# Wider products for the scores and for y in a chunked RWKV-7 kernel, and a refit of its scheduler

## The chip, the cores and the metric

The kernel runs on one core of one Trainium2 chip. The metric is the device time of one execution in microseconds (us). Runs of a kernel spread by up to 3% here, so kernels are compared by ratios of fast runs that were timed in the same rounds on the same chip.

## The reference

Batch 4, 8 heads, 768 steps, 40 channels per head; then a feed-forward block over 3072 tokens, 320 to 2048 to 320.

```python
for t in range(S):
    y[:, :, t] = np.einsum('bhd,bhde->bhe', rt, state)
    Sa = np.einsum('bhde,bhe->bhd', state, at)
    state = (state * wt[:, :, None, :] - np.einsum('bhd,bhe->bhde', Sa, bt)
             + np.einsum('bhd,bhe->bhde', vt, kt))
# y as (3072, 320) is x
h = x @ w_in
out = (h / (1.0 + np.exp(-1.702 * h))) @ w_out
```

## The kernel before

The recurrence is solved in chunks of 64 steps. A *unit* is one chunk of two batches (16 heads); there are 24. Every product of a unit is f32 on quarters of the array (64 rows by 64 columns), four tiles side by side: `QUARTERS` names them. Each call of `mm` becomes two passes, and each pass is a weight load and a matmul, so four instructions: the 16 calls of `score_RV` in each of the 24 units are the 768 matmuls of ps_RV below, with 768 loads. "Weights" here means the stationary operand, `lhsT`.

For y, each unit makes score matrices: v against r (`score_RV`) and SA against r (`scores`; SA is the solution of the chunk's triangular system). Both are masked by DVE, and `read` multiplies them with the decayed k and b. In the same product come 40 columns for the state: v's own values and those of SA.

```python
def mm(o, lhsT, rhs, start):
    nc.tensor.matmul(o, lhsT, rhs, start=start, stop=True, skip_group_check=True)

def by_time(t):                     # cumulative sum by time
    ps, lw = psum(t, "ps_cum"), logw_of(i)
    for n in (1, 0):
        for b in BITS:
            u = b ^ n
            mm(ps[HALF[u], b, :160], incl[HALF[b]], lw[HALF[b], n * 160:(n + 1) * 160], True)

def score_RV(t):                    # v against r; ready early, long before y
    for e, b in product(BITS, BITS):
        for f, u in QUARTERS:
            o, j = (2 * e + b) * 64, 4 * u + 2 * e + b
            mm(ps[HALF[u], f, o:o + 64], rv[HALF[f], 1, j], rv[HALF[f], 0, j], o == 0)
# ... DVE masks it into RV

# ... level(n, b): six levels of the triangular solve; in the last one each quarter
# writes its own half, mm(ps[HALF[q], h, ...], ...), 40 columns

def scores(t):                      # SA against r
    for e, b in product(BITS, BITS):
        for f, u in QUARTERS:
            o = (2 * e + b) * 64
            mm(ps[HALF[u], f, o:o + 64], saT_of(i)[HALF[f], 4 * e + 2 * u + b], rT[HALF[f], 4 * u + 2 * e + b], o == 0)
# ... DVE masks it into M

def read(t):                        # y and the new state
    for b, f in product(BITS, BITS):
        o = (2 * b + f) * 104
        for m, w in ((RV_of(i), kh_of(i)), (M_of(i), bh_of(i))):
            for u, e in QUARTERS:
                mm(ps[HALF[e], u, o:o + 104], w[HALF[u], 4 * b + 2 * f + e], m[HALF[u], 4 * f + 2 * e + b],
                   o == 0 and w is kh_t[i % 2])
```

The matmuls of the feed-forward block (`ps_up`, `ps_down`) fill TensorE between the steps of the solve. A small scheduler in the host code orders all this before it is emitted. It simulates every engine and the fetch of TensorE's instructions (`FETCH` ns for 256 of them, more beside transfers: `BESIDE`), with a duration given for each task; the numbers such as `pe((4, 64))` are these durations and not hardware settings.

## Time and profile before

| | before |
|---|---|
| time, first 3 runs | 824.3, 842.7, 842.1 us |
| time, medians of four later sets (11 to 59 runs) | 829.7 to 836.2 us |
| profiled span | 826.5 us |
| TensorE passes (loads and matmuls each) | 24,192 |
| instruction fetches of TensorE | 190 |

The prediction shows the main lines of the page and says what each is for. Two more belong to the change. They are from the table of groups; the columns are line, engine, operation, output<-inputs, shape, count, then busy us, mean ns of one, and the idle time before them.

```profile
L270 PE MATMUL ps_RV<-rv 64*64 64x64 f32 x768 | 18.0, 227 | 3.4 <-issue 2.1 <-ACT G L498 1.3
L270 PE MATMUL ps_M<-rv,saT 64*64 64x64 f32 x768 | 16.8, 218 | 0.4 <-ACT saT L641 0.4
```

`64*64 64x64` says that the array is used as a tile of 64 rows by 64 columns, with 64 moving columns. The reader should not take the mean of 218 ns for a cost: four tiles overlap, and neighbours start 14.5 ns apart on average.

### The profile page before, as it was taken

The page shows a single profiled execution, that of the slowest core. Times are in us where ns is not written, and L with a number is a line of the kernel's source. Part 1 is how long each engine was busy: PE and PEld are TensorE (multiplying, and loading weights), DVE is VectorE, ACT ScalarE, POOL GpSimd, SP SyncE. Part 2 cuts the span into 40 slices and gives each one's busy share as a digit, 9 for nine tenths or more (in the row PEclk, how much of TensorE's full clock was granted, in tenths as well). Part 3 has the DMA queues.
Part 4 walks back from the last instruction along what each step waited for, and adds up shares of the span by engine and source line. Part 5 has one row for each costly group of instructions (what it writes and reads, how often), then busy time and mean ns, then how long its engine had stood idle before and what let it go on. Part 6 is the DMA issues. An engine that isn't in the chain of part 4 may idle for free.

```text
span 826.5 us, 51261 instructions
## 1 busy us (share of the span) xinstructions
PE 754.0 (91%) x24192; PEld 630.7 (76%) x24192; DVE 477.3 (58%) x757; ACT 368.8 (45%) x634; POOL 148.2 (18%) x208
## 2 busy tenths in 40 slices
PE   4764898999899998999998998999999999999997
PEld 3664788887787786889787777788789888778664
DVE  7479898745754645546556456566466566455100
ACT  4564754443436347346445435344256445233110
POOL 4020303321312302302203212022113022100000
PEclk9896999999999999999999999999999999999999
DMA  9935433332411512323323315134133223110100
GB/s 343 336 116 165 167 121 110 108 104 54 151 56 58 149 59 78 117 75 94 112 73 101 110 43 157 36 94 133 56 97 113 64 68 105 49 36 29 35 10 17
DMA packets 33018, 82.60 MB, mean 100 GB/s; under 512 B 5128, under 2 KB 11272, under 8 KB 31528
## 3 DMA queue, kind: packets, MB, share of 16 engines
q1 hardware_dynamic: 32808, 79.32, 30.2%
q8 instruction: 190, 3.11, 1.5%
q14 instruction: 20, 0.16, 0.1%
HBM read 71.43 MB, written 7.86 MB: 96 GB/s over the span
## 4 chain that ended last, share of the span: by engine, by line
PE 84%; ACT 5%; DVE 4%; issue 4%; DMA 2%; SPq 0%; POOL 0%; ACTq 0%; POOLq 0%
PE ps_up L270 24%; PE ps_down L270 23%; PE ps_level L270 18%; PE ps_y L270 5%; PE ps_N L270 2%; PE ps_NT L270 2%; PE ps_A L270 2%; PE ps_rz L270 1%; PE ps_saT L270 1%; PE ps_M L270 1%; PE ps_zT L270 1%; PE ps_Av L270 1%; PE ps_RV L270 1%; ACT g L835 1%; ACT W L714 1%
## 5 line engine op out<-in xcount | busy, mean ns | idle before, releaser
L270 PE MATMUL ps_up<-xT,w_sb 64*64 64x256 f32 x3840 | 271.1, 380 | 8.5 <-ACT g L835 3.4
L270 PE MATMUL ps_down<-w_sb,g 64*64 64x320 f32 x3072 | 244.0, 431 | 1.7 <-DVE ob L861 0.6
L270 PEld LDWEIGHTS ps_up<-xT,w_sb 64*64 64x64 f32 x3840 | 155.6, 134 | 32.6 <-issue 6.6
L270 PEld LDWEIGHTS ps_level<-W,E 64*64 64x64 f32 x5888 | 149.2, 134 | 29.6 <-ACT g L835 3.5
L714 ACT COPY W<-ps_level 128x672 f32<-128x672 f32 (+1 forms) x154 | 95.2, 621 | 164.2 <-PE ps_level L270 152.1
L270 PEld LDWEIGHTS ps_down<-w_sb,g 64*64 64x64 f32 x3072 | 123.1, 134 | 46.3 <-issue 2.4
L270 PE MATMUL ps_level<-W,E 64*64 64x64 f32 (+2 forms) x5888 | 146.6, 230 | 6.4 <-DVE E L704 1.7
L709 DVE TENSOR_TENSOR E<-twice,ps_level 128x512 f32<-128x512 f32 x120 | 81.5, 683 | 64.7 <-ACT W L714 54.1
L535 POOL TENSOR_TENSOR kh<-time,G 128x320 f32<-128x320 f32 x22 | 19.6, 891 | 454.8 <-issue 254.6
L270 PEld LDWEIGHTS ps_level<-W 64*64 64x64 f32 x2560 | 69.9, 142 | 20.9 <-issue 12.6
L270 PE MATMUL ps_level<-W 64*64 64x64 f32 (+2 forms) x2560 | 71.9, 243 | 14.1 <-issue 10.4
L835 ACT ACTIVATE g<-ps_up 128x1024 f32<-128x1024 f32 x48 | 49.2, 1025 | 60.0 <-PE ps_up L270 59.6
L799 POOL TENSOR_TENSOR x<-y,FT 128x128 f32<-128x128 f32 x84 | 48.0, 601 | 19.7 <-DMA b<-in_b 19.6
L693 DVE TENSOR_TENSOR W<-edge,ps_level 128x672 f32<-128x672 f32 x40 | 34.0, 851 | 23.7 <-PE ps_level L270 21.1
L270 PE MATMUL ps_y<-RV,kh 64*64 64x104 f32 x768 | 38.5, 263 | 9.6 <-DVE M L756 9.1
L861 DVE TENSOR_TENSOR ob<-ob,ps_down 128x320 f32<-128x320 f32 x24 | 11.6, 484 | 58.8 <-ACT ob L859 58.4
L270 PEld LDWEIGHTS ps_y<-RV,kh 64*64 64x64 f32 x768 | 30.7, 142 | 12.6 <-DVE M L756 9.5
L270 PE MATMUL ps_y<-M,bh 64*64 64x104 f32 x768 | 38.7, 263 | 0.2 <-issue 0.2
L714 DVE COPY W<-ps_level 128x672 f32<-128x672 f32 (+1 forms) x46 | 34.4, 750 | 6.7 <-PE ps_level L270 6.7
L527 POOL TENSOR_TENSOR ak<-ak,FT 128x512 f32<-128x512 f32 x21 | 28.2, 1341 | 27.1 <-DMA ak<-in_ak 16.2
L756 DVE TENSOR_TENSOR M<-ps_M,upper 128x512 f32<-128x512 f32 x24 | 16.5, 688 | 26.5 <-PE ps_M L270 26.4
L859 ACT COPY ob<-ps_down 128x320 f32<-128x320 f32 x24 | 10.2, 426 | 47.1 <-PE ps_down L270 46.9
(111 smaller groups left out, 1019.6 us busy)
## 6 DMA issues: line engine op xcount, KB each, us to landing
time<-in_time SPq DMA_DIRECT2D x24, 480.0 KB
RV<-in_v SPq DMA_DIRECT2D x24, 416.0 KB
xT<-x_dram SPq DMA_DIRECT2D x48, 160.0 KB
ak<-in_ak SPq DMA_DIRECT2D x44, 160.0 KB
rv<-in_rv SPq DMA_DIRECT2D x44, 160.0 KB
wc<-in_wc SPq DMA_DIRECT2D x24, 264.0 KB
extra<-in_w_out SPq DMA_DIRECT2D x4, 1024.0 KB
logw<-in_w SPq DMA_DIRECT2D x24, 160.0 KB
```

The source lines that it names most:

```text
L270: nc.tensor.matmul(o, lhsT, rhs, start=start, stop=True, skip_group_check=True)
L527: plan.add(R, {"DVE": 690.0, "POOL": 1270.0, "sbuf": True}, lambda t: of(t.engine).tensor_mul(ahT(), ahT(), FT_of(i)), reads=T("ak", "FT") ...
L535: plan.add(R + 4, {"POOL": 870.0, "DVE": 490.0, "sbuf": True}, lambda t, n=n, dst=dst: of(t.engine).tensor_mul(dst(i)[:, :, :D], by_head(t ...
L693: plan.add(key, dve(672), lambda t: nc.vector.tensor_sub(W_of(s + 1)[:, :, b], edge[:, :, b], item(t)[:, :, :, :168]), reads=T("edge"), wr ...
L709: plan.add(key, dve(512), lambda t: nc.vector.tensor_sub(E_of(es + 1)[:, :, b].rearrange("p h j (n t) -> p h (j n) t", n=2), wide(twice).t ...
L714: plan.add(key, any2(4 * (168 - lo)), lambda t: copy(t.engine)(W_of(s + 1)[:, :, b, :, lo:], item(t)[:, :, :, lo:168]), writes=keeps, pair ...
L756: plan.add(R + 4, dve(512), lambda t: nc.vector.tensor_tensor(M_of(i)[:, :, :64].rearrange("p (e j) t -> p e j t", e=2), psum(t, "")[:, :, ...
L799: of(t.engine).tensor_mul(x[:, b ^ u, b], y_of()[:, at], FT_of(i)[:, at])
L835: plan.add(-45, act(1024), lambda t: nc.scalar.activation(g_of(c * NQ + q).rearrange("p m r n -> p r m n"), psum(t, "").rearrange("p r (m ...
L859: plan.add(-45, any2(320), lambda t: copy(t.engine)(ob_of(serial), psum(t, "")[:, 0, :DM]), writes=[("ob", serial)], pair=("down", serial))
L861: plan.add(-45, dve(320), lambda t: nc.vector.tensor_add(ob_of(serial), ob_of(serial), psum(t, "")[:, 1, :DM]), reads=[("ob", serial)], wr ...
```

## The change

Its intent is fewer TensorE instructions. v and SA lie side by side in one tile (`rv`, three planes: r, v, SA), so one load of 128 columns makes both scores of a head. Their results land on the two halves of the partitions, so y becomes one product over 128 rows. For that, the last level has to write only to the upper half, and the decay G has to exist on both halves for both batches. v is loaded without zeros, and the scheduler's constants are fitted anew. The cut diff leaves out that the masks are re-laid, that k and b are decayed in one product of 640, and that `xT` has two buffers in place of three.

```diff
-    BLOCK, FETCH, BESIDE, AHEAD = 256, 3550.0, 0.4, 300.0
-    DELAY = {"PE": 300.0, ... "SP": 800.0}
-    LATENCY, RATE, SPREAD = 1200.0, 400.0, 1.3
+    BLOCK, FETCH, BESIDE, AHEAD = 256, 3550.0, 0.37, 300.0
+    DELAY = {"PE": 300.0, ... "SP": 1300.0}
+    LATENCY, RATE = 1200.0, 400.0
...
-    W_IN, W_OUT = 12, 30
+    W_IN, W_OUT = 12, 35
...
         def by_time(t):
-            for n in (1, 0):
-                for b in BITS:
-                    u = b ^ n
-                    mm(ps[HALF[u], b, :160], incl[HALF[b]], lw[HALF[b], n * 160:(n + 1) * 160], True)
+            for b, h in QUARTERS:
+                mm(ps[HALF[h], b, :DM], incl[HALF[b]], lw[HALF[b]], True)
...
-        def score_RV(t): ...            # removed
...
+                        if last:
+                            o = (2 * q + j) * 128
+                            mm(ps[HALF[1], h, o:o + D], E[HALF[h], q, j, 64:], w[HALF[h], q, j, 64:104], j == 0 and q == h)
+                            continue
...
         def scores(t):
-            for e, b in product(BITS, BITS):
-                for f, u in QUARTERS:
-                    mm(ps[HALF[u], f, o:o + 64], saT_of(i)[HALF[f], ...], rT[HALF[f], ...], o == 0)
-        plan.add(R + 4, pe((4, 64)), scores, ...)
+            for j, (b, e, u) in enumerate(product(BITS, BITS, BITS)):
+                for f in BITS:
+                    mm(ps[:, f, j * 64:(j + 1) * 64], rv[HALF[f], 4 * e + 2 * b + u, 1:].rearrange("p r t -> p (r t)"),
+                       rv[HALF[f], 4 * e + 2 * b + u, 0], j == 0)
+        plan.add(R + 4, {"PE": 930.0 + 290.0, "instr": 64}, scores, ...)
...
         def read(t):
-            for m, w in ((RV_of(i), kh_of(i)), (M_of(i), bh_of(i))):
-                for u, e in QUARTERS:
-                    mm(ps[HALF[e], u, o:o + 104], w[HALF[u], ...], m[HALF[u], ...], ...)
+            for b, f, u, e in product(BITS, BITS, BITS, BITS):
+                mm(ps[HALF[e], u, o:o + 104].rearrange("p (g n) -> p g n", n=8), kb_of(i)[:, 8 * b + head(e, f, b, u)],
+                   RM_of(i)[:, :, 8 * b + 4 * e + 2 * u + f], o == 0)
+        plan.add(R + 4, {"PE": 1435.0 + 290.0, "instr": 64}, read, ...)
```

More of the change, by code (lines that the diff above doesn't have):

```diff
@@ L59 @@
 class Plan:
-    BLOCK, FETCH, BESIDE, AHEAD = 256, 3550.0, 0.4, 300.0
-    DELAY = {"PE": 300.0, "DVE": 60.0, "ACT": 60.0, "POOL": 150.0, "SP": 800.0}
-    LATENCY, RATE, SPREAD = 1200.0, 400.0, 1.3
+    BLOCK, FETCH, BESIDE, AHEAD = 256, 3550.0, 0.37, 300.0
+    DELAY = {"PE": 300.0, "DVE": 60.0, "ACT": 60.0, "POOL": 150.0, "SP": 1300.0}
+    LATENCY, RATE = 1200.0, 400.0
     def __init__(self, slots, pairs):
@@ L125, in fetch @@
                 beside = sum(max(0.0, min(y, at + took) - max(x, at)) for x, y in running[-8:])
-                took = self.FETCH + self.BESIDE / self.SPREAD * beside
+                took = self.FETCH + self.BESIDE * beside
             return took
@@ L178, in order @@
                 wire = max(wire, end + self.LATENCY)
-                running.append((wire, wire + self.SPREAD * t.size / self.RATE))
+                running.append((wire, wire + t.size / self.RATE))
                 end = wire = running[-1][1]
@@ L248, in rwkv7_gelu_quick @@
     banks = ctx.enter_context(tc.tile_pool(name="banks", bufs=1, space=bass.MemoryType.PSUM))
-    plan = Plan(dict(logw=3, wc=3, G=1, wch=3, wz=2, time=2, ak=2, b=2, rv=2, FT=3, GT=1, kh=2, bh=2, bz=2,
-                     A=1, Av=1, RV=2, W=3, E=2, edge=1, zraw=2, zT=1, saT=1, M=2, y=1, x=1, xT=3, g=4, ob=1), 4)
+    plan = Plan(dict(logw=3, wc=3, G=1, wch=3, wz=2, time=2, ak=2, b=2, rv=2, FT=3, GT=1, kb=2, bz=2,
+                     A=1, Av=1, RM=2, W=3, E=2, edge=1, zraw=2, zT=1, saT=2, y=1, x=1, xT=2, g=4, ob=1), 4)
     tiles, psums, drams = {}, {}, {}
@@ L336, in several @@
         return [single(f"{name}{i}", shape) for i in range(plan.slots[name])]
-    kh_t, bh_t = several("kh", [128, 8, 64]), several("bh", [128, 8, 64])
-    for t in kh_t + bh_t:
+    kb_t = several("kb", [128, 16, 64])
+    for t in kb_t:
         nc.gpsimd.memset(t[:, :, D:], 0.0)
@@ L343, in rwkv7_gelu_quick @@
         nc.gpsimd.memset(t[:, DM:], 0.0)
-    ak_t, b_t, rv_t = several("ak", [128, 2, 8, 64]), several("b", [128, 8, 64]), several("rv", [128, 2, 8, 64])
+    ak_t, b_t, rv_t = several("ak", [128, 2, 8, 64]), several("b", [128, 8, 64]), several("rv", [128, 8, 3, 64])
     bz_t = several("bz", [128, 8 * 104 + 24])
@@ L420, in weights @@
             weight(n, W_IN + 0.4 * n if n < NK else W_OUT + 1.6 * (n - NK), w_in[n] if n < NK else w_out[n - NK])
-    time_of = lambda i: buf("time", i, [128, 3, DM])
+    time_of = lambda i: buf("time", i, [128, 3 * DM])
     ak_of, b_of, rv_of = lambda i: ak_t[i % 2], lambda i: b_t[i % 2], lambda i: rv_t[i % 2]
-    RV_of = lambda i: buf("RV", i, [128, 8, 104])
+    RM_of = lambda i: buf("RM", i, [128, 13, 16, 8])
     logw_of = lambda i: buf("logw", i, [128, DM])
@@ L437, in load, with go @@
         for name, of, src, n in (("ak", ak_of, ak_d, 1024), ("time", time_of, time_d, 3 * DM), ("b", b_of, b_d, 512),
-                                 ("rv", rv_of, rv_d, 1024), ("RV", RV_of, v_d, 832)):
+                                 ("rv", rv_of, rv_d, 1024), ("RM", RM_of, v_d, 640)):
             rows = [slice(p.start, p.start + D) for p in HALF] if i >= 2 and name in ("ak", "b", "rv") else [slice(0, 128)]
-            def go(t, of=of, src=src, rows=rows):
+            def go(t, name=name, of=of, src=src, rows=rows):
+                if name == "RM":
+                    nc.sync.dma_start(of(i)[HALF[0], 8:].rearrange("p g j n -> p (g j n)"), src[i])
+                    return
                 for p in rows:
-                    nc.sync.dma_start(of(i)[p], src[i, p])
-            plan.add(10 * i - 4, {"SP": 350.0 * len(rows)}, go, writes=[(name, i)] + ([("v", i)] if name == "RV" else []),
-                     size=sum(p.stop - p.start for p in rows) * n * 4)
-    G_of = lambda i: buf("G", i, [128, 2, 160])
+                    nc.sync.dma_start(of(i)[p, :, :2] if name == "rv" else of(i)[p], src[i, p])
+            plan.add(10 * i - 4, {"SP": 350.0 * len(rows)}, go, writes=[(name, i)],
+                     size=128 * n * (5.5 if name == "rv" else 2 if name == "RM" else 4))
+    G_of = lambda i: buf("G", i, [128, 2, DM])
     FT_of = lambda i: buf("FT", i, [128, 8, 64])
@@ L478, in by_time @@
             ps, lw = psum(t, "ps_cum"), logw_of(i)
-            for n in (1, 0):
-                for b in BITS:
-                    u = b ^ n
-                    mm(ps[HALF[u], b, :160], incl[HALF[b]], lw[HALF[b], n * 160:(n + 1) * 160], True)
-        plan.add(R, pe((1, 160)), by_time, reads=T("log"), uses=T("logw"), room=T("G"), writes=T("cum"), pair=("cum", i))
+            for b, h in QUARTERS:
+                mm(ps[HALF[h], b, :DM], incl[HALF[b]], lw[HALF[b]], True)
+        plan.add(R, pe((1, 320)), by_time, reads=T("log"), uses=T("logw"), room=T("G"), writes=T("cum"), pair=("cum", i))
         def exp_channel(t):
@@ L497, in decay @@
                  writes=T("FT", "GT", "wch"))
-        plan.add(R, {"ACT": 460.0}, lambda t: nc.scalar.activation(G_of(i), psum(t, "")[:, :, :160], ACT.Exp, scale=-1.0),
+        plan.add(R, {"ACT": 700.0}, lambda t: nc.scalar.activation(G_of(i), psum(t, "")[:, :, :DM], ACT.Exp, scale=-1.0),
                  reads=T("FT"), writes=T("G", "exps"), pair=("cum", i))
@@ L503, in decay @@
                      reads=T("wch") + [("wch", i - 2)], writes=T("wz"))
-    def by_head(t):
-        return t.rearrange("t (h d) -> t h d", h=H)
     A_of = lambda i: buf("A", i, [128, 8, 64])
@@ L513, in rwkv7_gelu_quick @@
     zraw_of = lambda i: buf("zraw", i, [128, 8, D])
-    saT_of = lambda i: buf("saT", i, [128, 8, 64])
-    M_of = lambda i: buf("M", i, [128, 8, 104])
     xT_of = lambda c: buf("xT", c, [128, 2, NK, 128])
-    kh_of, bh_of = lambda i: kh_t[i % 2], lambda i: bh_t[i % 2]
+    kb_of = lambda i: kb_t[i % 2]
     zT_of = lambda i: zT_t[i % plan.slots["zT"]]
@@ L523, in prep @@
         T = lambda *names: [(n, i) for n in names]
-        G = lambda: G_of(i).rearrange("t b (h d) -> t (b h) d", d=D)
         ahT, khT = (lambda: ak_of(i)[:, 0]), (lambda: ak_of(i)[:, 1])
@@ L533, in prep @@
                  reads=T("ak", "GT"), writes=T("khT"))
-        for n, (name, dst) in enumerate((("kh", kh_of), ("bh", bh_of))):
-            plan.add(R + 4, {"POOL": 870.0, "DVE": 490.0, "sbuf": True}, lambda t, n=n, dst=dst: of(t.engine).tensor_mul(
-                dst(i)[:, :, :D], by_head(time_of(i)[:, n]), G()), reads=T("time", "exps", "G"), writes=T(name))
+        plan.add(R + 4, {"POOL": 1700.0, "DVE": 830.0, "sbuf": True}, lambda t: of(t.engine).tensor_mul(
+            kb_of(i)[:, :, :D], time_of(i)[:, :2 * DM].rearrange("t (h d) -> t h d", d=D),
+            G_of(i).rearrange("t b (h d) -> t (b h) d", d=D)), reads=T("time", "exps", "G"), writes=T("kb"))
         def score_NT(t):
@@ L563, in times_v @@
         def times_v(t):
-            ps, v_b = psum(t, "ps_Av"), time_of(i)[:, 2]
+            ps, v_b = psum(t, "ps_Av"), time_of(i)[:, 2 * DM:]
             for e, f in product(BITS, BITS):
@@ L573, in prep @@
                  writes=T("Av"), pair=("Av", i))
-        def score_RV(t):
-            ps, rv = psum(t, "ps_RV"), rv_of(i)
-            for e, b in product(BITS, BITS):
-                for f, u in QUARTERS:
-                    o, j = (2 * e + b) * 64, 4 * u + 2 * e + b
-                    mm(ps[HALF[u], f, o:o + 64], rv[HALF[f], 1, j], rv[HALF[f], 0, j], o == 0)
-        plan.add(R + 9, pe((4, 64)), score_RV, reads=T("rv"), room=T("RV"), pair=("RV", i))
-        plan.add(R + 9, dve(512), lambda t: nc.vector.tensor_tensor(
-            RV_of(i)[:, :, :64].rearrange("p (e j) t -> p e j t", e=2), psum(t, "")[:, :, :256].rearrange("p e (j t) -> p e j t", t=64),
-            mask(upper), ALU.mult), reads=T("v"), writes=T("RV"), pair=("RV", i))
     def last_e(i):
@@ L682, in level @@
             wide = lambda t: t.unsqueeze(1).unsqueeze(1)
-            sets = [(2, 104 if n < LEVELS - 2 else 40)] + ([] if last else [(2, 64)]) + ([(1, 80)] if early and alone else [])
+            sets = [(2, 104 if n < LEVELS - 2 else 120 if last else 40)] + ([] if last else [(2, 64)]) + ([(1, 80)] if early and alone else [])
             key, pair = R + 1 + n * 0.5, (f"L{b}", s)
@@ L686, in level @@
                      uses=[("W", s)] + ([] if alone else [("E", es)]),
-                     room=T("M") if last else [("W", s + 1)] + ([] if early and n < LEVELS - 2 else [("E", es + 1)]), pair=pair)
+                     room=T("RM") if last else [("W", s + 1)] + ([] if early and n < LEVELS - 2 else [("E", es + 1)]), pair=pair)
             keeps = [(f"W{b}", s + 1), ("W", s + 1)]
@@ L698, in level @@
             elif last:
-                plan.add(key, any2(160), lambda t: signed(
-                    t, M_of(i).rearrange("p (f e b) n -> p b e f n", f=2, e=2)[:, b, :, :, 64:], item(t)[:, :, :, 64:104], i >= EARLY),
-                         writes=T("M"), pair=pair)
+                plan.add(key, any2(320), lambda t: signed(
+                    t, RM_of(i)[HALF[1], 8:, 8 * b:8 * b + 8].rearrange("p g j n -> p j g n"),
+                    psum(t, "")[HALF[1]].rearrange("p h (j n) -> p (h j) n", n=128)[:, :, :D].rearrange("p j (g n) -> p j g n", n=8),
+                    i >= EARLY), writes=T("RM"), pair=pair)
             else:
@@ L723, in sa_turned @@
             ps, w, E = psum(t, "ps_saT"), W_of(6 * i + 5), E_of(last_e(i))
-            for u, b in product(BITS, BITS):
+            for b, u in product(BITS, BITS):
                 for e, f in QUARTERS:
-                    o = (2 * u + b) * 64
+                    o = (2 * b + u) * 64
                     mm(ps[HALF[f], e, o:o + 64], w[HALF[e], u, b, f, 64:128], E[HALF[e], u, b, f, 64:], o == 0)
@@ L731, in solve @@
         plan.add(R + 4, any2(512), lambda t: signed(
-            t, saT_of(i).rearrange("p (r j) t -> p r (j t)", r=2), psum(t, "")[:, :, :256], i >= EARLY), writes=T("saT"), pair=("saT", i))
+            t, rv_of(i)[:, :, 2].rearrange("p (e j) t -> p e j t", e=2),
+            psum(t, "")[:, :, :256].rearrange("p e (j t) -> p e j t", t=64), i >= EARLY), writes=T("saT"), pair=("saT", i))
         y_of, x_of = lambda: buf("y", i, [128, 8, 64]), lambda: buf("x", i, [128, 4, 2, 64])
@@ L736, in read_state @@
             def read_state(t):
-                ps, rT = psum(t, "ps_rz"), rv_of(i)[:, 0]
+                ps, rT = psum(t, "ps_rz"), rv_of(i)[:, :, 0]
                 for u, b in product(BITS, BITS):
@@ L741, in read_state @@
                         o, at = (2 * u + b) * 64, (4 * e + 2 * u + b) * D
-                        mm(ps[HALF[e], f, o:o + 64], zT_of(i)[HALF[f], at:at + 64], rT[HALF[f], 4 * u + 2 * e + b], o == 0)
+                        mm(ps[HALF[e], f, o:o + 64], zT_of(i)[HALF[f], at:at + 64], rT[HALF[f], 4 * e + 2 * b + u], o == 0)
             plan.add(R + 6, pe((4, 64)), read_state, reads=T("rv", "zT"), room=T("y"), pair=("rz", i))
@@ L748, in scores @@
         def scores(t):
-            ps, rT = psum(t, "ps_M"), rv_of(i)[:, 0]
-            for e, b in product(BITS, BITS):
-                for f, u in QUARTERS:
-                    o = (2 * e + b) * 64
-                    mm(ps[HALF[u], f, o:o + 64], saT_of(i)[HALF[f], 4 * e + 2 * u + b], rT[HALF[f], 4 * u + 2 * e + b], o == 0)
-        plan.add(R + 4, pe((4, 64)), scores, reads=T("saT", "rv"), room=T("M"), pair=("M", i))
-        plan.add(R + 4, dve(512), lambda t: nc.vector.tensor_tensor(
-            M_of(i)[:, :, :64].rearrange("p (e j) t -> p e j t", e=2), psum(t, "")[:, :, :256].rearrange("p e (j t) -> p e j t", t=64),
-            mask(upper), ALU.mult), writes=T("M"), pair=("M", i))
+            ps, rv = psum(t, "ps_M"), rv_of(i)
@@ new lines, in scores @@
+            for j, (b, e, u) in enumerate(product(BITS, BITS, BITS)):
+                for f in BITS:
+                    mm(ps[:, f, j * 64:(j + 1) * 64], rv[HALF[f], 4 * e + 2 * b + u, 1:].rearrange("p r t -> p (r t)"),
+                       rv[HALF[f], 4 * e + 2 * b + u, 0], j == 0)
+        plan.add(R + 4, {"PE": 930.0 + 290.0, "instr": 64}, scores, reads=T("saT", "rv"), room=T("RM"), pair=("M", i))
+        for f in BITS:
+            plan.add(R + 4, dve(512), lambda t, f=f: nc.vector.tensor_tensor(
+                RM_of(i)[:, :8].rearrange("p g (j f) n -> p f j g n", f=2)[:, f],
+                psum(t, "")[:, f].rearrange("p (j g n) -> p j g n", j=8, g=8),
+                upper.rearrange("p (g n) -> p g n", n=8).unsqueeze(1).to_broadcast([128, 8, 8, 8]), ALU.mult),
+                     writes=T("RM"), pair=("M", i))
@@ L760, in read @@
         def read(t):
             ps = psum(t, "ps_y")
-            for b, f in product(BITS, BITS):
+            for b, f, u, e in product(BITS, BITS, BITS, BITS):
                 o = (2 * b + f) * 104
-                for m, w in ((RV_of(i), kh_of(i)), (M_of(i), bh_of(i))):
-                    for u, e in QUARTERS:
-                        mm(ps[HALF[e], u, o:o + 104], w[HALF[u], 4 * b + 2 * f + e], m[HALF[u], 4 * f + 2 * e + b],
-                           o == 0 and w is kh_t[i % 2])
-        plan.add(R + 4, pe((8, 104)), read, reads=T("RV", "M", "kh", "bh") + (T("rz") if c > 0 else []), room=T("y", "zraw"),
-                 pair=("y", i))
+                mm(ps[HALF[e], u, o:o + 104].rearrange("p (g n) -> p g n", n=8), kb_of(i)[:, 8 * b + head(e, f, b, u)],
+                   RM_of(i)[:, :, 8 * b + 4 * e + 2 * u + f], o == 0)
@@ L772, in part @@
+        plan.add(R + 4, {"PE": 1435.0 + 290.0, "instr": 64}, read, reads=T("RM", "kb") + (T("rz") if c > 0 else []),
+                 room=T("y", "zraw"), pair=("y", i))
         def part(t):
@@ L813, in get_back @@
                 nc.sync.dma_start(xT_of(c)[h, p].rearrange("q k n -> q (k n)"), drams[i].rearrange("(q k) n -> q (k n)", q=64))
-        plan.add(-50, {"SP": 700.0}, part_with, reads=T("x"), writes=T("xd"), size=DM * 512)
+        plan.add(-50, {"SP": 700.0}, part_with, reads=T("x"), writes=T("xd"), size=DM * 512 * 1.6)
         plan.add(-50, {"SP": 700.0}, get_back, reads=T("xd"), writes=[("xT", c), ("xs", (c, p))], size=2 * DM * 512)
@@ L905, with by_batch, time_tile, both @@
     units = [(c, p) for c in range(NC) for p in range(B // 2)]
-    def time_tile(x, swapped):
-        x = np.asarray(x, np.float32).reshape(B, H, NC, C, D)
-        t = np.empty((len(units), 2, C, H, D), np.float32)
-        for n, (c, p) in enumerate(units):
-            for half in range(2):
-                for slot in range(2):
-                    if swapped:
-                        hs = 4 * (slot ^ half)
-                        t[n, half, :, 4 * slot:4 * slot + 4] = x[2 * p + slot, hs:hs + 4, c].transpose(1, 0, 2)
-                    else:
-                        t[n, half, :, 4 * slot:4 * slot + 4] = x[2 * p + half, 4 * slot:4 * slot + 4, c].transpose(1, 0, 2)
-        return t.reshape(len(units), 128, H * D)
+    def by_batch(x):
+        x = np.asarray(x, np.float32).reshape(B // 2, 2, H, NC, C, D).transpose(3, 0, 1, 4, 2, 5)
+        return x.reshape(len(units), 2, C, H, D)
+    def time_tile(x):
+        return by_batch(x).reshape(len(units), 128, H * D)
+    def both(x):
+        return by_batch(x).transpose(0, 2, 1, 3, 4).reshape(len(units), C, 2 * H * D)
     def channel_tile(x, half, order):
@@ L935, in beside @@
         x = np.asarray(x, np.float32).reshape(B, H, NC, C, D)
-        t = np.zeros((len(units), 2, C, 8, C + D), np.float32)
+        t = np.empty((len(units), C, D // 8, 16, 8), np.float32)
         for n, (c, p) in enumerate(units):
             for e, f, b, u in product(range(2), repeat=4):
-                t[n, u, :, 4 * f + 2 * e + b, C:] = x[2 * p + b, e + 2 * f + 4 * (b ^ u), c]
-        return t.reshape(len(units), 128, 8, C + D)
+                t[n, :, :, 8 * b + 4 * e + 2 * u + f] = x[2 * p + b, e + 2 * f + 4 * (b ^ u), c].reshape(C, D // 8, 8)
+        return t.reshape(len(units), C, 16 * D)
     def halves(t):
@@ L956 @@
     arrays = {
-        "in_time": np.ascontiguousarray(np.stack([time_tile(k, True), time_tile(b, True), time_tile(v, False)], 2)),
+        "in_time": np.concatenate([np.concatenate([both(k), both(b)], 1), time_tile(v)], 2),
         "in_v": beside(v),
-        "in_w": time_tile(w, False),
+        "in_w": np.ascontiguousarray(time_tile(w)),
         "in_wc": halves(channel_tile(w, "e", "ubf")),
@@ L962 @@
         "in_b": channel_tile(b, "e", "ubf"),
-        "in_rv": np.ascontiguousarray(np.stack([channel_tile(r, "f", "ueb"), channel_tile(v, "f", "ueb")], 2)),
+        "in_rv": np.ascontiguousarray(np.stack([channel_tile(r, "f", "ebu"), channel_tile(v, "f", "ebu")], 3)),
         "in_w_in": np.ascontiguousarray(w_in),
```

## The prediction

> **What bounds the kernel now.** I read the page first: busy table, slices, chain by engine, DMA queues.
>
> ```profile
> PE 754.0 (91%) x24192; PEld 630.7 (76%) x24192; DVE 477.3 (58%) x757; ACT 368.8 (45%) x634; POOL 148.2 (18%) x208
> ...
> PE   4764898999899998999998998999999999999997
> ...
> q8 instruction: 190, 3.11, 1.5%
> ...
> PE 84%; ACT 5%; DVE 4%; issue 4%; DMA 2%; SPq 0%; POOL 0%; ACTq 0%; POOLq 0%
> ```
>
> TensorE is the bound from about 140 us on; no other engine is near it. It reads 48,384 instructions (each f32 product is two passes, each pass a weight load and a matmul), and the queue line shows how they come: in 190 fetches, 3.11 MB, so 16 KiB or 256 instructions each. In the trace the starts of these fetches lie 3.9 us apart in the median, 3.4 us at the lowest tenth. TensorE needs about as long to use a block up, so there are two bounds side by side: array time and fetch.
>
> The windows table says where TensorE is not full:
>
> ```profile
> 0.00:70.00 70.00, 38.83 (x1472) 35.26 (x1472) 48.53 (x75) 36.49 (x64) 14.25 (x31) 0.91 0.68 247
> 70.00:140.00 70.00, 59.34 (x2008) 53.39 (x2012) 61.86 (x79) 40.50 (x64) 19.26 (x20) 0.89 0.46 148
> 140.00:759.00 619.00, 593.16 (x19444) 501.09 (x19440) 359.69 (x590) 279.83 (x489) 114.68 (x157) 0.99 0.29 87
> 759.00:827.00 68.00, 62.70 (x1284) 40.98 (x1276) 7.24 (x16) 11.98 (x19) 0.00 (x0) 0.99 0.08 21
> ```
>
> For array time I take durations from the timeline, start of one set to start of the next:
>
> ```profile
> 159.90 0.68 PE L270 MATMUL ps_RV<-rv 64*64 64x64 f32 x32
> 160.36 1.07 PE L270 MATMUL ps_up<-xT,w_sb 64*64 64x256 f32 x16
> ```
>
> So 32 passes of 64 columns take 0.46 us: 14.5 ns each, four tiles of the array sharing 58 ns. The same reading gives 22.3 ns for a pass of 104 columns (64 in 1.43 us, the ps_y pieces of the chain) and 67.5 ns for 320 columns (16 in 1.08 us, ps_down). With these,[...] all 24,192 passes sum to **712 us** of pure array time. Walking the starts of all matmuls with those costs leaves 91 us in which the array had nothing queued: 50 us before 140 us, 40 us between 140 and 759. When I number TensorE's instructions, 32 of the 81 us in the larger of these gaps fall into one sixteenth of the 256 positions of a block: these are waits for **fetch**. The waits view shows the same under "issue":
>
> ```profile
> PE ps_level L270 <- issue: 11.8, 10, 3.5
> PE ps_y L270 <- DVE M L756: 9.1, 1, 9.1
> ```
>
> The second line is start-up: DVE, converting weights, was late with a mask once.
>
> [...]every form on the page is 64*64. [...]The trace has only 64-column loads (134 ns recorded, overlapped). [...]the 128x512 masks (687 and 688 ns) agree, so I expect the re-laid masks to cost the same.
>
> **The change part by part**, per unit (24 units).
>
> Fewer instructions. v's score product, 32 passes, disappears into the one of SA; y goes from 64 passes to 32. That is 64 passes, 128 instructions per unit, 3,072 in all: 12 fetches fewer, 178.
>
> Scores. Before: two products of 32 passes, 2 x 0.464 = 0.93 us. After: 32 passes with 128 loaded columns on two row tiles, not four: if a tile's pass still takes 58 ns, 16 x 58 = 0.93 us, the same. [...]I take the first, which is also the entry in the scheduler's table, with 0.29 us for switching the tiling: **+0.29 us**.
>
> y. Before 64 x 22.3 = 1.43 us on four tiles; after 32 passes on two tiles of 128 rows, 44.7 ns each, again 1.43, with a switch: **+0.29 us**.
>
> Last level. All its outputs now go to the upper half of the partitions, so two tiles work instead of four: 2 x 16 passes go from 0.46 us to 0.82 (the table's 51.5 ns per pair of passes): **+0.36 us**.
>
> Cumulative sum by time. Every half now needs both batches: 8 passes of 320 columns in place of 160, 0.54 for 0.27: **+0.27 us**.
>
> Sum +1.21 us per unit, **+29 us**: array time 741 us.[...]
>
> Other engines: the exponent of G doubles (0.42 to about 0.70 us on ACT), the last level's copy becomes 64x320 (0.29 to about 0.43, twice), GpSimd does one product of 640 for two of 320. All these engines are under 60% busy, so this is hidden, except that v's mask, formerly made early, now stands in the chain SA, scores, two masks, y: about +2 us of latency per unit. After 140 us the MLP's matmuls fill that; before, it may cost 3 to 6 us.
>
> DMA: the 416 KB load of v becomes 160 KB, 6.1 MB less in all of 79, but r and v land in pieces of 512 B. DMA is at 0.29 in the steady part; nothing waits for these loads there.
>
> **What fetch gives back.** In the steady part a block holds 3.77 us of array time and takes 4.07. Blocks with 3 to 3.5 us of work take 3.81: there fetch binds. After the change a block has 741/177 = 4.19 us of work on average, above the usual fetch. I expect fetch stalls to go from 32 to 12 us: **-20 us**. In start-up, where issue is a third of the chain between 20 and 50 us, that is part of it. The refit picture of fetch and transfers, and later w_out loads, may win the scheduler some of the remaining 58 us of stalls: **-10 us**, a guess. Sum: 826.5 + 29 - 20 - 10 + 3 = 828.
>
> **Rivals.** (1) Fetch is the true bound: 12 fetches x 3.9 us = 47 us less, with the array's extra time absorbed: 790 to 805. For it: fetches nearly back to back. Against it: 712 us of array time in 826, and 84% of the chain on TensorE. (2) Array time becomes the only bound, with wide loads and four switches per unit dearer than the table says: 845 to 860. [...]against it: the table's new entries look fitted to measurements. (3) All is hidden in the schedule's noise, 820 to 835; the runs of before already spread from 824 to 843.
>
> **Range and chances.** The steps give 828. I shade it to 826 since the slower runs of before (842) look like slower fetch, to which the new kernel is less exposed, though the same spread may appear. Against the median of 842 that is 1.9% faster, against the fast runs nothing. Range 806 to 846. Faster 0.33, same 0.58, slower 0.09.
>
> **What would show it.** Fetch: 178 fetches, with medians above 4.1 us apart, and less "issue" on TensorE. Scores: 32 passes of the 128-column form within about 0.93 us (right)[...]. Switches: gaps of about 0.3 us around ps_M and ps_y. TensorE's share should rise from 91% to 93% or more. The prediction is wrong if the array's added time is far from 29 us, or if the new order leaves TensorE more or less idle before 140 us than now[...].

## The result, and the profile after

The changed kernel took **846.63 us** in the median of 4 runs (846.4 to 848.0), against 834.78 (824.3 to 842.7) of before. The ratio is **1.0254** (95% interval 1.0216 to 1.0293). A ratio compares the fast runs alone, in the same rounds, so it is not the ratio of the medians. Fast means within 1.5% of the fastest run of the same kernel: for the kernel before, whose runs spread widely, that leaves out 2 of the 4 runs here, for the changed kernel none. A second set gave 1.0234 (e11, below; 5 of 11 runs of before left out). The change is slower by 2.3 to 2.5% in fast runs; the medians of all runs give 1.4 and 2.0%. The median of 846.63 lies just above the predicted range.

These are the page's busy table, its fetch queue and its chain of waits by engine, after the change:

```profile
PE 793.4 (94%) x22656; PEld 632.6 (75%) x22656; DVE 470.8 (56%) x751; ACT 376.9 (45%) x632; POOL 141.6 (17%) x190
...
q8 instruction: 178, 2.92, 1.4%
...
PE 80%; ACT 8%; DVE 5%; issue 3%; DMA 2%; SPq 1%; ACTq 0%; DVEq 0%
```

The intent was met: 1,536 passes and 12 fetches fewer (3,072 loads and matmuls, so 256 to a fetch). Yet TensorE is busy 39 us longer, with 6% fewer matmuls. The windows table has the same four stretches as in the prediction (the columns are the stretch, its length, busy us and count of PE, PEld, DVE, ACT and POOL, then the granted clock, the DMA share and GB/s):

```profile
0.00:70.00 70.00, 43.28 (x1344) 37.56 (x1344) 49.92 (x75) 36.52 (x61) 17.27 (x31) 0.84 0.68 231
70.00:140.00 70.00, 62.06 (x1882) 52.63 (x1882) 58.06 (x78) 40.84 (x62) 17.64 (x17) 0.92 0.43 138
140.00:759.00 619.00, 606.84 (x17860) 487.45 (x17864) 351.94 (x579) 283.47 (x487) 106.69 (x142) 1.00 0.27 78
759.00:845.00 86.00, 81.24 (x1594) 55.00 (x1584) 10.90 (x22) 16.09 (x23) 0.00 (x0) 0.99 0.08 22
```

Up to 140 us nothing was lost: passes worth 82 us of array time had started by then, against 77 before. From 140 to 759 us the array was fuller than before (607 of 619 us, then 593) but got through 17,860 passes, not 19,444. What was left ran after 759 us.

The groups of the two sets that replaced four, after the change:

```profile
L271 PEld LDWEIGHTS ps_M<-rv 64*128 64x128 f32 x768 | 45.8, 191 | 7.7 <-issue 2.9
L271 PE MATMUL ps_M<-rv 64*128 64x64 f32 x768 | 49.2, 279 | 0.7 <-ACT rv L626 0.7
...
L271 PE MATMUL ps_y<-RM,kb 128*64 128x104 f32 x768 | 40.9, 261 | 1.9 <-DVE RM L749 1.5
```

ps_M, with half the matmuls of the two sets that it replaced, is busy 49.2 us; those two were busy 18.0 and 16.8. A piece of the timeline gives the cost of one set, as start to start (columns: start, us, engine, line, operation, count):

```profile
301.32 2.00 PE L271 MATMUL ps_M<-rv 64*128 64x64 f32 x32
303.25 0.82 PE L271 MATMUL ps_level<-W 64*64 64x104 f32 x32
```

32 passes take 303.25 - 301.32 = 1.93 us; the median over all units is 1.93 too. Before, two sets of 0.46 us did this work. Inside a set, passes on the same row tile start 112 ns apart, in loads and in matmuls: 56 ns for each of the 32, or 1.79 us of the 1.93.

**The account.** As in the prediction, I sum the pure array time of all passes and walk their starts for stalls (gaps over 60 ns). Widths for which the prediction gives no cost take, start to start in the trace of before, 17.6 ns (80 columns), 34.2 (160) and 54.1 (256). The costs of the new forms are 56 ns for each pass of 128 loaded columns, as measured above; 44.8 for each of 128 rows (44.5 in the trace); and 25.8 for the last level, half of the 51.5 that the prediction takes from the scheduler's table (its measured 0.437 us over 16 passes, 27.3 ns each, would make the array time 1 us more). Medians of the sets in the traces, from a set's first start to the next set's, per unit:

| per unit, us | before | after | measured change | predicted |
|---|---|---|---|---|
| scores, v and SA | 0.93 | 1.93 | +1.00 | +0.29 |
| y | 1.43 | 1.58 | +0.15 | +0.29 |
| last level (two sets) | 2 x 0.204 | 2 x 0.437 | +0.47 | +0.36 |
| cumulative sum by time | 0.27 | 0.54 | +0.27 | +0.27 |
| sum | | | +1.89 | +1.21 |
| 24 units | | | +45 | +29 |

| whole kernel, us | before | after |
|---|---|---|
| array time without changes of tiling | 712 | 748 |
| stalls in all | 91 | 72 |
| of these, before 140 us | 50 | 45 |
| of these, at the fetch position of the block | 32 | 16 |
| short stalls (up to 0.3 us) at ps_M and ps_y | 3 | 12 |

A set's time from start to start holds the change of tiling that ends it, but not the one that begins it: that one lengthens the set before. It can be read from the trace after the change:

```profile
205.30 1.26 PE L271 MATMUL ps_down<-w_sb,g 64*64 64x320 f32 x16
206.49 1.65 PE L271 MATMUL ps_y<-RM,kb 128*64 128x104 f32 x32
```

16 passes of 320 columns take 1.08 us before another set of 64*64, and 206.49 - 205.30 = 1.19 here. In the median ps_y began 0.11 us late (15 sets that follow ps_up or ps_down) and ps_M 0.25 us (12 sets); the scores of e1 below, on 64*64 again, began with no delay. So y costs 0.15 + 0.11 = 0.26 us more per unit, and the scores about 1.25.

In the walk, array time rose by 36.0 us, the short stalls at ps_M and ps_y (mostly changes of tiling) by 9, the other stalls fell by 18.7 + 9 = 27.7, and gaps too short to be counted grew by 1.2: 18.5 us in all, as between the two profiles. That sum is no test, since the walk shares out the whole time. It is a model on the recorded starts, not something that the profile states.

### The profile page after: what moved, and what is told of

Its sections match the earlier page's. It is cut to its first block, busy times and chain, and to the rows that moved or that the text cites. A ratio compares the mean times of both kernels' runs of the same rounds, so it can differ in the third digit from the quotient of the medians.

```text
span 845.0 us, 48221 instructions
## 1 busy us (share of the span) xinstructions
PE 793.4 (94%) x22656; PEld 632.6 (75%) x22656; DVE 470.8 (56%) x751; ACT 376.9 (45%) x632; POOL 141.6 (17%) x190
## 3 DMA queue, kind: packets, MB, share of 16 engines
q1 hardware_dynamic: 45384, 73.03, 28.4%
## 4 chain that ended last, share of the span: by engine, by line
PE 80%; ACT 8%; DVE 5%; issue 3%; DMA 2%; SPq 1%; ACTq 0%; DVEq 0%
PE ps_down L271 23%; PE ps_up L271 21%; PE ps_level L271 16%; PE ps_M L271 5%; PE ps_y L271 4%; PE ps_N L271 2%; ACT L828 1%; PE ps_saT L271 1%; PE ps_NT L271 1%; PE ps_zT L271 1%; ACT g L828 1%; PE ps_Av L271 1%; DMA extra<-in_w_in 1%; PE ps_cum L271 1%; PE ps_rz L271 1%
## 5 line engine op out<-in xcount | busy, mean ns | idle before, releaser
L271 PE MATMUL ps_up<-xT,w_sb 64*64 64x256 f32 x3840 | 254.8, 379 | 4.4 <-ACT g L828 2.8
L271 PEld LDWEIGHTS ps_up<-xT,w_sb 64*64 64x64 f32 x3840 | 141.5, 133 | 40.8 <-ACT g L828 4.0
L531 POOL TENSOR_TENSOR kb<-time,G 128x640 f32<-128x640 f32 x22 | 35.4, 1611 | 454.9 <-issue 326.3
L271 PEld LDWEIGHTS ps_level<-W 64*64 64x64 f32 x2560 | 65.8, 143 | 21.4 <-issue 8.5
L828 ACT ACTIVATE g<-ps_up 128x1024 f32<-128x1024 f32 x48 | 49.2, 1024 | 57.4 <-PE ps_up L271 56.9
L749 DVE TENSOR_TENSOR RM<-ps_M,upper 128x512 f32<-128x512 f32 x48 | 30.9, 685 | 49.9 <-PE ps_M L271 49.9
L271 PEld LDWEIGHTS ps_M<-rv 64*128 64x128 f32 x768 | 45.8, 191 | 7.7 <-issue 2.9
L271 PE MATMUL ps_M<-rv 64*128 64x64 f32 x768 | 49.2, 279 | 0.7 <-ACT rv L626 0.7
L271 PEld LDWEIGHTS ps_y<-RM,kb 128*64 128x64 f32 x768 | 36.0, 140 | 9.2 <-issue 7.3
L271 PE MATMUL ps_y<-RM,kb 128*64 128x104 f32 x768 | 40.9, 261 | 1.9 <-DVE RM L749 1.5
L568 ACT COPY Av<-ps_Av 128x320 f32<-128x320 f32 x23 | 9.8, 425 | 51.4 <-PE ps_Av L271 51.3
```

Source lines behind the costliest of these rows:

```text
L531: plan.add(R + 4, {"POOL": 1700.0, "DVE": 830.0, "sbuf": True}, lambda t: of(t.engine).tensor_mul(kb_of(i)[:, :, :D], time_of(i)[:, :2 * D ...
L568: plan.add(R + 1, any2(320), lambda t: copy(t.engine)(Av_of(i).rearrange("p e b n -> p b e n"), psum(t, "")[:, :, :160].rearrange("p b (e ...
L749: plan.add(R + 4, dve(512), lambda t, f=f: nc.vector.tensor_tensor(RM_of(i)[:, :8].rearrange("p g (j f) n -> p f j g n", f=2)[:, f], psum( ...
L828: plan.add(-45, act(1024), lambda t: nc.scalar.activation(g_of(c * NQ + q).rearrange("p m r n -> p r m n"), psum(t, "").rearrange("p r (m ...
```

## The experiments

The theory after the result, A: the scores' 128-column loads, mis-sized in the prediction, carry the loss. The rivals: the new order of work or the refit picture does; the longer chain through masks and copies does; or the scheduler's wrong duration of the scores does. Twelve runs were made; all gave correct results. In the "stalls" of the runs below the same walk is meant.

### e1_split: the same scores on four tiles of 64 columns

```diff
-                for f in BITS:
-                    mm(ps[:, f, j * 64:(j + 1) * 64], rv[HALF[f], 4 * e + 2 * b + u, 1:].rearrange("p r t -> p (r t)"),
+                for f, g in QUARTERS:
+                    mm(ps[HALF[g], f, j * 64:(j + 1) * 64], rv[HALF[f], 4 * e + 2 * b + u, 1 + g],
                        rv[HALF[f], 4 * e + 2 * b + u, 0], j == 0)
```

The scheduler's durations are left alone, so the order of everything else is the same.

> The changed kernel in the same order, but each 128-column score product issued as two of 64 columns on the four 64x64 tiles (64 passes instead of 32, 64 instructions per unit more, 6 fetches more, two changes of tiling per unit fewer). Theory A (the scores are what was mis-sized: 1.93 us per unit in the profile where 1.22 was predicted): the set takes 0.93 us, 24 us of array time go away, fetch takes some 5 to 8 back, span about 845 - 24 + 7 = 828, ratio to before 1.00 to 1.01. Rival B (fetch was all the time the smaller matter and the new order of work is what costs): the set gets shorter but the time stays within 6 us of 845, ratio 1.02 or more.

Median 837.75 us of 13 runs, **ratio 1.0065** (1.0024 to 1.0105), span 829.2 us. The timeline and the groups of e1_split:

```profile
452.85 1.03 PE L271 MATMUL ps_M<-rv 64*64 64x64 f32 x57
453.67 0.38 PE L271 MATMUL ps_up<-xT,w_sb 64*64 64x256 f32 x1
```

```profile
L271 PE MATMUL ps_M<-rv 64*64 64x64 f32 x1536 | 30.9, 219 | 1.7 <-issue 0.9 <-ACT rv L626 0.7
```

57 passes begin and end in about 0.8 us; the median of a set is 0.94 us, counted where 59 of its 64 passes run together. Twice the passes of the changed kernel are busy 18 us less. Array time falls from 748 to 727 us, stalls rise from 72 to 78. Of the 2.5% lost, 1.9 points go with this one edit (each ratio is against before, from its own rounds; by medians of all runs 1.2 of 1.4), so theory A holds, and the rival (little change) falls. The edit takes away the wide loads and the two changes of tiling around them together; the pitch inside a set (1.79 of 1.93 us, against 0.94 for the whole set here) says that the loads are the larger part.

### e3_halved: load the 128 columns twice, stream 32 columns each time

```diff
+                for q in BITS:
                     for f in BITS:
-                    mm(ps[:, f, j * 64:(j + 1) * 64], ..., rv[HALF[f], 4 * e + 2 * b + u, 0], j == 0)
+                        o = j * 64 + 32 * q
+                        mm(ps[:, f, o:o + 32], ..., rv[HALF[f], 4 * e + 2 * b + u, 0, 32 * q:32 * q + 32], j == 0 and q == 0)
```

In the trace after, a load starts 56 ns after a matmul of its row tile and the next matmul 56 ns after the load. That could be a load that takes the whole pitch of 112 ns, or a load and a stream of some 56 ns each, one after the other. This kernel was meant to separate them.

> The changed kernel in the same order, each score product split along its moving side: the same 128 columns are loaded twice, each time for a moving operand of 32 columns (64 passes). It tells two mechanisms of the slow scores apart. H1, a load of 128 columns [...]sets the pitch by itself: the pitch per pass stays 112 ns on a row tile, the set takes about 3.6 us, 1.7 us per unit or 41 us more, span about 880 to 890. H3, load (53 ns) and streaming (56 ns) of a row tile merely run one after the other: the pitch falls to about 53 + 30 = 83 ns, the set takes about 2.7 us, 0.8 us per unit or 19 us more, span about 860 to 868.

The timeline of e3_halved:

```profile
463.34 3.87 PE L271 MATMUL ps_M<-rv 64*128 64x32 f32 x64
467.14 1.13 PE L271 MATMUL ps_up<-xT,w_sb 64*64 64x256 f32 x8
```

The set takes 3.8 us here, 3.69 in the median, and the pitch on a row tile is 112 ns as before, though it streams half the columns. This fits H1: **the load of 128 columns sets the pitch, and streaming hides under it**. If 32 columns took as long to stream as 64, H3 would leave the pitch at 112 too, and no run times such a stream alone. Against that stand the records of the loads, with a median of 188 ns for 128 columns against 135 for 64: 53 ns for 64 more columns. That is about what the pitch on a row tile grew by, from 58 to 112 ns.

The total was a miss: median 919.16, ratio 1.1084 (1.0978 to 1.119), span 918.0 where 880 to 890 was expected. The set accounts for 24 x 1.76 = 42 of the 73 us above the changed kernel. The windows of e3_halved show another part in the third column from the right, the granted clock:

```profile
140.00:350.00 210.00, 206.70 (x5756) 169.02 (x5758) 119.15 (x195) 91.72 (x158) 35.08 (x45) 0.95 0.26 77
350.00:560.00 210.00, 202.97 (x5648) 165.44 (x5641) 108.45 (x176) 90.82 (x153) 33.68 (x44) 0.97 0.27 77
560.00:780.00 220.00, 216.59 (x5992) 174.92 (x5988) 110.42 (x185) 88.89 (x155) 32.82 (x44) 0.96 0.23 67
```

It is 1.00 after the change in such stretches. In the trace the clock went to half for 3.4 or 6.8 us 14 times between 100 and 850 us, each time between 3.2 us before and 0.9 us after the end of a ps_M set. 0.05 x 210 + 0.03 x 210 + 0.04 x 220 = 26 us of full clock are missing, by an estimate from these lines. In the timeline above, the 8 passes of ps_up just after the set take 0.90 us (the next set starts at 468.04); 8 of them take 0.43 in the median of the traces of before and after. Why the clock fell is not shown: the kernel before has two such falls (at 286 and 437 us, 3.4 us each) without wide loads, and the changed kernel, with sets of 1.93 us, has none between 85 and 842 us. The last 5 us stay open; the stretch before 140 us, with a clock of 0.83 against 0.88, isn't in this sum.

### e2_oldpic and e4_before_newpic: the scheduler's picture alone

e2 is the changed kernel with the old constants and transfer sizes; e4 is the kernel before with the new ones.

```diff
-    BLOCK, FETCH, BESIDE, AHEAD = 256, 3550.0, 0.37, 300.0
+    BLOCK, FETCH, BESIDE, AHEAD = 256, 3550.0, 0.4, 300.0      # e2; e4 the other way round
```

> The changed kernel with the scheduler's old constants and old transfer sizes; the emitted work is the same, only its order differs. Theory A: the picture matters by less than 1%, 838 to 852 us, ratio 1.015 to 1.035. Rival B (the refit order is the cause of the loss): back to 832 or less, ratio 1.01 or less.

> The kernel before with the scheduler's new constants and transfer sizes alone. Theory A: within 1% of before, ratio 0.99 to 1.01. Rival B: it is 1.5% or more slower, which would lay part of the loss on the refit picture.

e2: median 847.99, ratio 1.0237 (1.0189 to 1.0285). e4: median 831.59, ratio **0.9998** (0.9966 to 1.0029). The refit picture is worth nothing that shows to either kernel, in gain or loss (the intervals are 0.3 to 0.5% wide to each side), though it reorders most of TensorE's stream.

### e5_last4 and e6_cum160: the other two array costs

Both start from e1. e5 gives the last level its four tiles back and moves the results to the upper half in the copy (the order of heads in `RM` follows):

```diff
-                            o = (2 * q + j) * 128
-                            mm(ps[HALF[1], h, o:o + D], ...)
+                            o = j * 256
+                            mm(ps[HALF[q], h, o:o + D], ...)
...
+                for q in BITS:                 # two copies, each half of the partitions to the upper half
+                    plan.add(key, any2(160), ...)
```

e6 takes the cumulative sum at 160 columns, as before the change, and lets ACT write each exponent to both halves:

```diff
+            for u, h in QUARTERS:
+                nc.scalar.activation(G[HALF[h], 0:4:3] if u == 0 else G[HALF[h], 1:3], psum(t, "")[HALF[u], :, :160], ACT.Exp, scale=-1.0)
```

> The split scores of e1, and the last level's products back on four tiles, their results moved to the upper half of the partitions by the copy (two copies of 64x160 for one of 64x320). In the profiles 16 passes of the last level took 0.204 us before and 0.437 after, twice per unit: 0.47 us, 11 us in all. Theory A (array time lost to two-tile sets is the rest of the loss): 8 to 11 us less than e1, ratio 0.993 to 1.000. Rival B (the rest is the longer chain through the masks and copies, not array time): no gain, since the chain gets a copy longer, ratio 1.003 to 1.012.

> The split scores of e1, and the cumulative sum by time back at 160 columns, the exponent writing each result to both halves (four ACT instructions of 64x320 in place of one of 128x640). It takes 0.27 us per unit off TensorE, 6 us in all, and puts about 1 us on ACT, which is 45% busy. Theory A: 3 to 6 us less than e1, ratio 0.998 to 1.004. Rival B (ACT's place in the chain matters more than TensorE's array time): no change or slower, ratio 1.005 to 1.015.

e5: median 834.31 of 22 runs, ratio **1.0068** (1.0043 to 1.0094), so nothing against e1, as its rival B said; theory A's gain of 8 to 11 us failed to show. e6: median 831.67, ratio 1.0023 (0.999 to 1.0055), within theory A, though the interval touches e1's. Why did e5 give nothing? Its last level is back at 0.204 us and its array time fell by 9 us (727 to 718), but stalls rose by 10 (78 to 89), 6 of them at the fetch position. I cannot say from this run alone whether fetch took it back or the new order or the extra copy did.

### e9_last4c and e8_all: with the real durations in the scheduler

e9 is e5 with the scheduler told what scores and y take; e8 adds e6's edit.

```diff
-        plan.add(R + 4, {"PE": 930.0 + 290.0, "instr": 64}, scores, ...)
+        plan.add(R + 4, pe((8, 64)), scores, ...)
-        plan.add(R + 4, {"PE": 1435.0 + 290.0, "instr": 64}, read, ...)
+        plan.add(R + 4, {"PE": 1435.0 + 150.0, "instr": 64}, read, ...)
```

> e5 with the scheduler told what the sets really take (scores 0.93 us and 128 instructions, y 1.58 us, last level on four tiles), so its order differs. Theory A: a few us below e5 or the same, ratio 0.985 to 1.000. Rival B (the order is noise): within 0.5% of e5 to either side.

> All three: split scores, last level on four tiles, cumulative sum at 160 columns, with the real costs in the scheduler. Array time is then that of before but for two changes of tiling around y (0.15 us per unit, 4 us), and TensorE reads 64 instructions per unit less than before (6 fetches, of which the stalls before suggest 5 to 10 us). Theory A: ratio 0.980 to 0.998. Rival B (ACT's extra 1 us and the longer chain eat it): 0.998 to 1.010.

e9: median 831.25, ratio 1.0023 (0.9993 to 1.0054). e8: median 829.42 of 22 runs, ratio **0.997** (0.9949 to 0.9991), the only interval of the study below 1. e9 just missed its range, e8 met it. With all array costs undone but y's changes of tiling, what stays of the change is y over 128 rows, 6 fetches fewer, v without zeros, the longer chain through masks and copies, and `xT` with one buffer fewer: 2.5 us gained, too little to be sure of in runs that spread by 3%. So the rival of the longer chain falls: e8 keeps it, one copy longer still, and loses nothing. Its array time is 712 us and its stalls are 91, just as before: fewer fetches did not mean fewer stalls.

### e10_told, e12_told_again, e11_after_again, e7_costs: the wrong entry

The scheduler believed 1.22 us of the scores, which took 1.93. e10 and e12 are the changed kernel with that entry, and y's, put right; e11 is the changed kernel beside e12 on one chip; e7 is e1 with right entries.

```diff
-        plan.add(R + 4, {"PE": 930.0 + 290.0, "instr": 64}, scores, ...)
+        plan.add(R + 4, {"PE": 1930.0, "instr": 64}, scores, ...)
```

> The changed kernel, with the scheduler told what the scores (1.93 us) and y (1.58 us) really take, in place of 1.22 and 1.72; the emitted work is the same. Theory A (array time itself is the loss): 840 to 850 us, ratio 1.015 to 1.03. Rival B (the wrong entry, by misplacing other work, made the loss): 835 or less, ratio 1.01 or less.

> The changed kernel as it is, once more, on the same chip as the next run, so that the two can be compared directly: 844 to 850 us, ratio to before 1.018 to 1.028.

> The same as e10 (real costs of scores and y told to the scheduler), beside the changed kernel on one chip. If the wrong entry cost time, it is 3 to 6 us below the changed kernel here too; if e10's 5 us were the difference between chips and shares of slow runs of before, within 2 us of it.

> e1 (split scores) with the scheduler told the real costs of scores and y. From e9 against e5 (0.45% better when told): 2 to 5 us below e1, ratio 1.000 to 1.005. If the order is noise: within 0.3% of e1 to either side.

e10: 841.49, ratio 1.0141 (1.0073 to 1.0208), just below what theory A expected. e11: 848.56, 1.0234 (1.0208 to 1.0261). e12: 844.36, 1.0177 (1.013 to 1.0225). On one chip the right entry gains about 4 us, 848.56 to 844.36, though the intervals overlap a little. So the wrong entry is a small part of the loss and the array time the larger. e7: median 836.31, ratio 1.0096 (1.0066 to 1.0125), no better than e1: telling the scheduler the truth does not always help. Differences of 0.3% between orders are not to be explained one by one.

## Why the prediction was wrong

**The step that failed** is the scores: "if a tile's pass still takes 58 ns, 16 x 58 = 0.93 us, the same." It takes 112 ns, since the load of 128 columns binds (e3: same pitch with half the stream; and the records of the loads). The set took 1.93 us, not 1.22: 0.71 us per unit, 17 us in all. 828 + 17 = 845, the profiled span, though only because the other errors below nearly cancel. Rival 2 named dearer wide loads, but the sum was built on the entry in the scheduler's table. The prediction took that entry for a measurement ("look fitted to measurements"); the trace doesn't bear it out.

**Rival 2** is what happened: array time is the bound, with wide loads dearer than the table says (1.93 us a set, not 1.22). It named 845 to 860. Its other half, dearer changes of tiling, holds at the scores (0.25 us before the set and 0.14 in it, for the 0.29 of the table), but not at y.

**Other terms of the array sum.** y was about right, 0.26 us for 0.29, with both of its changes of tiling counted. The last level was undersized by 0.11: it took 0.87 us, not 0.82, and before it 0.41, not 0.46, since its passes of 40 columns take 12.7 ns (0.204 us for 16), not the 14.5 of 64 columns. The cumulative sum was right. The starts at a change of tiling were late by 0.11 and 0.25 us, and on time where the tiling stayed (the scores of e1).

**What fetch and the order give back.** "-20 us" for fetch: stalls at the fetch position fell by 16. "-10 us, a guess" for the picture: e2 and e4 show that the picture gives nothing. Yet stalls other than the changes of tiling did fall by 28 us, near the 30 of both terms together. The total was right by luck, since its split was wrong; 5 us of the fall lie before 140 us, where "+3" was expected.

**Fewer fetches are not time by themselves.** The idea behind "-20 us" was a block with more array time in it than a fetch takes. The traces agree: starts of fetches went from 3.9 us apart to 4.3 in the median (the lowest tenth was 3.5 before, not the 3.4 of the prediction), so the array, not fetch, sets the pace after the change. The gain was paid for with array time, and at 1.89 us per unit or more that was dearer than the stalls it hid. e5 shows the other side: there, 9 us of array time taken away came back as 10 us of stalls.

**The signs named for the steps** came out so: 178 fetches with a median above 4.1 us, TensorE at 94%, gaps at ps_M and ps_y, and a set of scores of 1.93 us, where 0.93 was named as right. The load of v without zeros was not tried alone; the main queue moves 6.3 MB less (79.3 to 73.0), in more and smaller packets (45,384 for 32,808), and no run shows a gain from it.

**The shading** from 828 to 826, for slow runs of before, was a mistake of too few runs: the four larger sets put the median of before at 830 to 836, not at 842, and no run shows that its slow runs are slow in fetch.

## What to carry to other kernels

Before making a product wider to save instructions, time the weight load of the wider form, and count the tiles that work at once: two row tiles of 128 columns, with 64 moving columns, took 1.93 us for the scores that four tiles of 64 made in 0.94. When instruction fetch and array time lie close together, work out both per block of instructions: 12 fetches fewer gained nothing here where the array had more to do, and in e5 9 us less array time gained nothing either. A duration in a host-side scheduler is a claim to be checked in the trace, not evidence.
